# A recurrent-memory attention kernel with feed-forward: the memory rows turned by VectorE block transposes in place of TensorE matmuls

## The chip, the cores and the metric

The kernel runs on one core of one Trainium2 chip. A core has TensorE (PE in the profile; its weight loads are PEld), VectorE (DVE), ScalarE (ACT), GpSimd (POOL) and SyncE (SP), which issues most of the transfers. Each engine works through its own instructions in order, and semaphores make one wait for another. The metric is the device time of one execution in microseconds (us), the median of several runs.

## The reference, cut to what matters

Attention runs over 64 segments of 32 tokens. Ahead of each segment stand 8 memory rows, which are the first 8 output rows of the segment before: a recurrence. A feed-forward part follows.

```python
B, S, Dm = 1, 2048, 640; H, Dh = 32, 128; M, seg = 8, 32
mask = (idx[:, None] < M) | (idx[:, None] >= idx[None, :])
mem = mem0
for s in range(64):
    h = concat([mem, x[:, s*32:(s+1)*32]], axis=1)          # 40 rows
    q, k, v = h @ Wq, h @ Wk, h @ Wv                        # 32 heads of 128
    p = softmax(where(mask, q @ k.T * Dh**-0.5, -1e9))
    o = (p @ v) @ Wo
    mem = o[:, :M]                                          # 8 rows to the next segment
    outs.append(o[:, M:])
h  = x + A(layernorm(x))
h2 = h + (relu(layernorm(h) @ w1 + b1)**2 @ w2 + b2)
```

Only the 8 memory rows tie a segment to the next.

## The kernel before

One step of the main loop (`step(b, sp)`, four to a block `b` of 128 tokens) handles one segment. 24 of its 32 tokens ("main") share a stationary tile with the 8 memory rows: `hT4` holds, for each of the 5 chunks of 128 features and each of the 4 segments of a block, 32 columns, first 8 memory rows, then 24 main tokens. The other 8 tokens of a segment ("tail") are collected over 16 segments and projected in units (`tail_units`) that are put into gaps: the list `fill` holds such units (a unit is 4 matmuls), and `run(fill, n)` issues n of them. The lists `late`, `mid` and `win` hold other work for three places of a step. The order is written by hand; every engine follows it.

A step goes so:

- Projections of queries and keys for 16 heads at a time (`project`, `proj`, L204). ScalarE evacuates a product (`row`), VectorE turns it in 32x32 blocks (`flip`, L225, L396) into `qT` and `kT`. `qT` has 40 columns for each head: 8 memory queries, 24 main, 8 tail.
- `spread` (L362, L364) copies on POOL the memory queries out of `qT` into `qz`; the memory queries' scores (`scores`, L409) read `qz`. The token scores (`token_scores`, L485) read the columns `M:NK` of `qT`: main and tail queries.
- Projection of the values, the softmax of the memory scores (`soft1`, `soft2`, with the transpose `pTm`, L428), then the values of the tokens of the step before (`token_values`) and of this step's memory queries (`values`, L437 and L442), evacuated to `oT` by `values_out` (L211, L213).
- The place `win`: in the fourth step of a block (`sp == 3`) `ln_transpose` turns the 128 rows of the block after the next with five 128x128 matmuls (L179), and ScalarE copies them to a new `hT4` (L190). Then two `fill` units, the token softmax, and `wo_rounds` (L236), 64 matmuls with `oT` as stationary tile into `pw`.
- ScalarE copies half of `pw` (`otmp`, L243), VectorE adds both halves (`o`, L244): 8 memory rows and, below them, 24 main rows of the step before, for both halves of the output's columns (partitions 0 to 31 and 32 to 63). `wov2` picks the columns that go to each half: pieces of 64.
- Five more `fill` units, then `mem_to_hT` (L305): 20 small matmuls against the identity turn the memory rows into `pm` (L308), and VectorE copies `pm` to the first 8 columns of the next segment's tile (`hT`, L310). `tails_in` copies on POOL the next segment's tail queries into `qT` (L314) and its tail keys into `kT` (L315).
- `mid`, the rest of `fill`, and the transposes `pTt` (L555) and `pTk` (L561) of the token softmax for the next step. Then the next step's projections, whose stationary tile is `hT`.

`store_main` writes the main rows to DRAM (L330). The first step is different: its projections are streamed with the arriving weights (`start`), and its tail values `vt` are loaded by POOL's queue (L326). The feed-forward part follows the loop.

Of the kernel before, what the change touches and what calls it, by code (L numbers as in the profile page):

```python
# [16 lines left out]
def kernel(  # L17
# [16 lines left out]
    nc = tc.nc  # L34
# [49 lines left out]
    nc.gpsimd.affine_select(out=mask[0:32], in_=mask[0:32], compare_op=ALU.is_ge, fill=NEG, base=0,  # L84
# [13 lines left out]
    qT = const.tile([128, H, NK], BF16)  # L98
# [31 lines left out]
    for o in o_ring:  # L130
        nc.gpsimd.memset(o[64:128], 0.0)
# [3 lines left out]
    for ch in range(2):  # L135
        nc.sync.dma_start(out=o0[32 * ch:32 * ch + M, :].rearrange("m (c f) -> m c f", f=64),
                            in_=A_mem0[0].rearrange("m (c t f) -> t m c f", t=2, f=64)[ch])
# [22 lines left out]
    hT4s, hTts, tails = {}, {}, {}  # L160
# [13 lines left out]
    def ln_transpose(b):  # L174
# [6 lines left out]
        def out():  # L181
# [6 lines left out]
            hT4 = s2.tile([128, DC, 4, SEG], BF16, tag="hT4", name="hT4")  # L188
            ptv = pt[:, 0:640].rearrange("p (c s t) -> p c s t", c=DC, s=4)
            nc.scalar.copy(out=hT4[:, :, :, M:SEG], in_=ptv[:, :, :, 0:HD])  # L190
            hT4s[b] = hT4
# [35 lines left out]
    wov2 = wo[:].rearrange("p h (c t f) -> p h t c f", t=2, f=64)  # L227
# [76 lines left out]
    def mem_to_hT(o, hT4, sp):  # L304
        pm = chn.tile([128, 512], F32, tag="ch", name="pm")  # L305
        for c in range(DC):
            for q in range(4):
                nc.tensor.matmul(pm[32 * q:32 * q + 32, c * M:(c + 1) * M], lhsT=o[:, (2 * c + q % 2) * 32:(2 * c + q % 2 + 1) * 32],  # L308
                                 rhs=ident[:, q // 2 * 32:q // 2 * 32 + M], start=True, stop=True)
        nc.vector.tensor_copy(out=hT4[:, :, sp, 0:M], in_=pm[:, 0:DC * M].rearrange("p (c m) -> p c m", m=M))  # L310

    def tails_in(b, sp):
        q, k = [tails[b][w][:].rearrange("p h (k s) -> p h s k", s=4)[:, :, sp, :] for w in "qk"]
        nc.gpsimd.tensor_copy(out=qT[:, :, SEG:NK], in_=q)  # L314
        nc.gpsimd.tensor_copy(out=kT[:, :, SEG:2 * SEG].rearrange("p h (j k) -> p h j k", k=TL),  # L315
                              in_=k.unsqueeze(2).to_broadcast([128, H, 4, TL]))

# [10 lines left out]
    def store_main(o, s):  # L328
        for ch in range(2):
            nc.sync.dma_start(out=o_all[s * SEG:s * SEG + HD, ch * DH:(ch + 1) * DH],  # L330
                              in_=o[32 * ch + M:32 * ch + 32, :])
# [4 lines left out]
    def token_values(s, v, vt4, po):  # L336
# [8 lines left out]
        for u in range(2):  # L345
            for g in range(G):
                r = slice(32 * g, 32 * g + 32)
                nc.tensor.matmul(po[:, g, u * 128:(u + 1) * 128].rearrange("p (j q) -> p j q", q=32)[:, :, HD:32],
# [19 lines left out]
    def step(b, sp, v=None):  # L368
# [82 lines left out]
        if not last and not ready:  # L451
            spread(0)
# [419 lines left out]
```

## Time and profile before

| | |
|---|---|
| median of 3 runs | 1040.73 us (1040.03 to 1041.76) |
| span of the profiled execution | 1035.5 us |
| mean granted TensorE clock in it | 0.993 |
| first projection after the first step's end to that after the 63rd | 70.18 to 886.12 us |
| a plain step | 12.85 us |

The span runs from the first to the last instruction. A row of a timeline gives start, duration, engine, line and operation; x is the number of instructions merged into it, and brackets hold how long the engine was idle before and what released it. A row of a group gives line, engine, operation, out<-in, shapes and count, then busy time in us, the mean of one in ns, and the idle time before it. These groups belong to the parts that the diff touches:

```profile
L308 PE MATMUL pm<-ident,o 128*32 128x8 bf16 x1280 | 18.6, 169 | 13.1 <-DVE o L244 12.3
L310 DVE CAST hT<-pm 128x40 bf16<-128x40 f32 x64 | 12.7, 199 | 27.4 <-PE pm L308 27.4
L314 POOL COPY qT<-qTt 128x256 bf16<-128x256 bf16 x64 | 27.5, 430 | 0.8 <-DVE qTt L225 0.8
L362 POOL COPY qz<-qT 128x96 bf16<-128x96 bf16 x126 | 33.4, 265 | 125.0 <-DVE qT L225 121.5 <-DVE mx L415 3.6
L179 PE MATMUL pt<-ident,xn 128*128 128x128 bf16 x100 | 10.0, 234 | 10.9 <-DVE xn L170 8.6 <-ACT row L220 2.1
L190 ACT COPY hT<-pt 128x480 bf16<-128x480 bf16 x16 | 8.7, 543 | 5.3 <-PE pt L179 5.3
```

### The profile page before, as it was taken

The page shows a single profiled execution, that of the slowest core. Times are in us where ns is not written, and L with a number is a line of the kernel's source. Part 1 is how long each engine was busy: PE and PEld are TensorE (multiplying, and loading weights), DVE is VectorE, ACT ScalarE, POOL GpSimd, SP SyncE. Part 2 cuts the span into 40 slices and gives each one's busy share as a digit, 9 for nine tenths or more (in the row PEclk, how much of TensorE's full clock was granted, in tenths as well). Part 3 has the DMA queues.
Part 4 walks back from the last instruction along what each step waited for, and adds up shares of the span by engine and source line. Part 5 has one row for each costly group of instructions (what it writes and reads, how often), then busy time and mean ns, then how long its engine had stood idle before and what let it go on. Part 6 is the DMA issues. An engine that isn't in the chain of part 4 may idle for free.

```text
span 1035.5 us, 58905 instructions
## 1 busy us (share of the span) xinstructions
PE 980.1 (95%) x26960; PEld 563.9 (54%) x26960; DVE 621.6 (60%) x1740; ACT 536.0 (52%) x1225; POOL 312.3 (30%) x805
## 2 busy tenths in 40 slices
PE   5879899999999999999999999999999998999998
PEld 2335455555655555555555655555555555555565
DVE  2155666766566666666666666666666676565432
ACT  2435555555555555555555555555555555534431
POOL 1033333333333333332333233333333333343210
PEclk9889999999999999999999999999999999999999
DMA  8960101000100000000000000000000110612200
GB/s 319 405 205 26 22 7 31 7 24 6 32 10 22 15 24 24 16 20 14 26 15 22 15 27 15 22 15 27 15 21 8 47 33 7 194 54 72 77 26 26
DMA packets 39112, 51.58 MB, mean 50 GB/s; under 512 B 6160, under 2 KB 34960, under 8 KB 36944
## 3 DMA queue, kind: packets, MB, share of 16 engines
q1 hardware_dynamic: 38000, 47.30, 13.8%
q8 instruction: 210, 3.44, 1.4%
q14 instruction: 38, 0.31, 0.1%
q10 hardware_dynamic: 544, 0.26, 0.1%
q0 software_dynamic: 320, 0.26, 0.1%
HBM read 38.37 MB, written 9.44 MB: 46 GB/s over the span
## 4 chain that ended last, share of the span: by engine, by line
PE 83%; DMA 6%; DVE 5%; issue 3%; ACT 2%; POOL 0%; SPq 0%; DVEq 0%; ACTq 0%; POOLq 0%
PE ps L204 45%; PE pw L236 13%; PE y L823 6%; PE ps L791 5%; PE ps L236 3%; DMA xt<-in_A_x_dram 3%; PE po L437 2%; PE pm L308 2%; PE sm L409 2%; DMA wq<-in_B_w_dram 1%; PE po L343 1%; PE ps L485 1%; ACT em L418 1%; DMA vt_d<-row 1%; DVE o L244 1%
## 5 line engine op out<-in xcount | busy, mean ns | idle before, releaser
L204 PEld LDWEIGHTS <-hT 128*32 128x32 bf16 x7680 | 186.9, 96 | 180.8 <-DVE hT L310 19.6
L204 PE MATMUL ps<-wv,hT 128*32 128x512 bf16 x2520 | 169.9, 379 | 0.7 <-ACT v L492 0.7
L236 PE MATMUL pw<-wo,oT 128*32 128x320 bf16 x4224 | 159.6, 300 | 3.3 <-DVE pTt L555 1.2
L204 PE MATMUL ps<-wq,hT 128*32 128x512 bf16 x2520 | 158.1, 380 | 4.8 <-DVE hT L310 4.8
L204 PE MATMUL ps<-wk,hT 128*32 128x512 bf16 x2520 | 157.6, 379 | 0.0
L236 PEld LDWEIGHTS <-oT 128*32 128x32 bf16 x4224 | 109.3, 97 | 50.7 <-DVE oT L211 15.8
L535 POOL TENSOR_TENSOR pkt<-ek,rk 128x64 bf16<-128x64 bf16 x64 | 18.8, 294 | 377.6 <-DVE rk L533 377.6
L220 ACT ACTIVATE row<-ps 128x512 bf16<-128x512 f32 x156 | 91.9, 601 | 78.4 <-PE ps L204 74.6
L225 DVE STREAM_TRANSPOSE qT<-row 128x512 bf16<-128x512 bf16 x128 | 90.6, 709 | 51.9 <-ACT row L220 51.9
L222 ACT CAST row<-ps 128x512 bf16<-128x512 f32 x115 | 65.9, 596 | 34.3 <-PE ps L204 34.3
L315 POOL COPY kT<-kTt 128x1024 bf16<-128x1024 bf16 x64 | 70.9, 1108 | 13.7 <-DVE kTt L225 13.7
L362 POOL COPY qz<-qT 128x96 bf16<-128x96 bf16 x126 | 33.4, 265 | 125.0 <-DVE qT L225 121.5
L353 ACT CAST oT<-po 128x512 bf16<-128x512 f32 x128 | 68.7, 589 | 1.6
L244 DVE TENSOR_TENSOR o<-pw,otmp 64x320 bf16<-64x320 f32 x66 | 31.8, 482 | 61.9 <-ACT otmp L243 61.9
L204 PEld LDWEIGHTS <-hTt 128*32 128x32 bf16 x1920 | 48.8, 99 | 35.6 <-issue 9.9
L225 DVE STREAM_TRANSPOSE kT<-row 128x512 bf16<-128x512 bf16 x65 | 46.0, 708 | 31.1 <-ACT row L222 31.1
L243 ACT COPY otmp<-pw 64x320 f32<-64x320 f32 x66 | 27.9, 422 | 70.9 <-PE pw L236 70.9
L823 PE MATMUL y<-wq,wk 128*128 128x320 bf16 x416 | 60.9, 299 | 0.0
L393 ACT CAST row<-ps 128x256 bf16<-128x256 f32 x126 | 40.7, 375 | 29.1 <-PE ps L204 29.0
L531 DVE TENSOR_REDUCE zk<-ek 128x8 f32<-128x320 bf16 x64 | 31.1, 486 | 40.2 <-ACT ek L527 40.2
L527 ACT ACTIVATE ek<-tk 128x320 bf16<-128x320 f32 x64 | 30.1, 470 | 45.1 <-DVE tk L525 45.1
L418 ACT ACTIVATE em<-sm,mx 128x64 bf16<-128x64 f32 x126 | 40.4, 321 | 24.3 <-DVE mx L415 24.3
(114 smaller groups left out, 1657.5 us busy)
## 6 DMA issues: line engine op xcount, KB each, us to landing
wv<-in_A_Wv_dram SPq DMA_DIRECT2D x5, 1024.0 KB
wq<-in_A_Wq_dram SPq DMA_DIRECT2D x5, 1024.0 KB
wk<-in_A_Wk_dram SPq DMA_DIRECT2D x5, 1024.0 KB
wo<-in_A_Wo_dram SPq DMA_DIRECT2D x4, 1280.0 KB
vt<-vt_d SPq DMA_DIRECT2D x60, 64.0 KB
xt<-in_A_x_dram SPq DMA_DIRECT2D x20, 160.0 KB
vt_d<-row SPq DMA_DIRECT2D x22, 128.0 KB
wq<-in_B_w_dram SPq DMA_DIRECT2D x1, 2080.0 KB
```

The source lines that it names most:

```text
L204: nc.tensor.matmul(ps[32 * k:32 * k + 32, :], lhsT=lhs(c), rhs=wr[:, c, n, k], start=(c == 0), stop=(c == DC - 1))
L220: nc.scalar.mul(out=row, in_=ps, mul=scale)
L222: nc.scalar.copy(out=row, in_=ps)
L225: nc.vector.transpose(out=dst[:, n * 16:(n + 1) * 16, 0:32], in_=row.rearrange("p (h e) -> p h e", e=32))
L236: nc.tensor.matmul(pw[32 * j:32 * j + 32, 0:DH], lhsT=lhs(p), rhs=wov2[:, head(p), ch], start=(h == 0), stop=(h == 15))
L244: nc.vector.tensor_tensor(out=o[0:64], in0=pw[0:64, 0:DH], in1=tmp[0:64], op=ALU.add)
L315: nc.gpsimd.tensor_copy(out=kT[:, :, SEG:2 * SEG].rearrange("p h (j k) -> p h j k", k=TL), in_=k.unsqueeze(2).to_broadcast([128, H, 4, TL]))
L353: nc.scalar.copy(out=oTg[:, n, :, :, M:NK], in_=po[:, :, n * 128:(n + 1) * 128].rearrange("p g (j q) -> p g j q", q=32))
L393: nc.scalar.copy(out=row[:, u * 256:(u + 1) * 256], in_=ps[:, u * 256:(u + 1) * 256])
L418: nc.scalar.activation(out=em[:], in_=sms[n][:, 0:2 * SEG], func=ACT.Exp, bias=mx[:, 0:1], scale=1.0, accum_out=zm[:])
L791: nc.tensor.matmul(ps[:], lhsT=w1[:, c, fc * 128:(fc + 1) * 128], rhs=hnT[:, c, :], start=(c == 0), stop=(c == DC - 1))
L823: nc.tensor.matmul(y[:, hh, 0:DH], lhsT=f1T[:, fc, k * 128:(k + 1) * 128], rhs=w2[:, fc, cs], start=(fc == 0), stop=False, skip_group_chec ...
```

## The change

- The stationary tiles of all blocks become one tile `hTall`, with an offset of 24 columns: for each chunk of features two blocks of four segments of 32 columns (8 memory, 24 main). `mem_to_hT` now runs straight behind `o` and consists of two VectorE transposes of 64 partitions by 160 elements, one for each half of a chunk's 128 partitions. Each writes 32 columns in every chunk: the 8 memory columns of the next segment and the 24 columns ahead of them, which hold the main tokens of the segment that has just been worked through.
- For that the rows of `o` are in another order: 24 main rows, then 8 memory rows, and its columns are dealt to the two halves in pieces of 32. `wo_rounds` therefore reads the columns `M:NK` of `oT`, `oT` keeps the memory columns last, `wov2`, `prep_sum`, `store_main` and the load of `mem0` follow.
- Tail queries take the memory queries' place in `qT`, which shrinks to 32 columns: `tails_q_in` copies them on POOL for 16 heads at a time, behind `spread`. The mask and the positions in `pTt`, `po` and `oT` follow (tail queries first, then main).
- Since the transposes overwrite main columns, `ln_transpose` for the next block moves from the fourth step of a block to the first step of the one after, and that of the tail rows from a first step to a second.
- The five memsets of `o`'s lower half go, as nothing reads it any more.

```diff
     nc.vector.memset(mask[:], 0.0)
-    nc.gpsimd.affine_select(out=mask[0:32], in_=mask[0:32], compare_op=ALU.is_ge, fill=NEG, base=0,
+    nc.gpsimd.affine_select(out=mask[0:32], in_=mask[0:32], compare_op=ALU.is_ge, fill=NEG, base=-TL,
+                            pattern=[[0, HG], [-1, SEG]], channel_multiplier=1)
+    nc.gpsimd.memset(mask[0:TL], 0.0)
+    nc.gpsimd.affine_select(out=mask[0:TL], in_=mask[0:TL], compare_op=ALU.is_ge, fill=NEG, base=HD,
                             pattern=[[0, HG], [-1, SEG]], channel_multiplier=1)
...
     nc.vector.tensor_scalar(out=bmask[:], in0=same[:], scalar1=-1.0, scalar2=-NEG, op0=ALU.add, op1=ALU.mult)
-    qT = const.tile([128, H, NK], BF16)
+    qT = const.tile([128, H, SEG], BF16)
+    hTall = const.tile([128, HD + DC * 2 * 4 * SEG], BF16, name="hTall")
     kT = const.tile([128, H, 2 * SEG], BF16)
...
     o_ring = [const.tile([128, DH], BF16, name="o%d" % k) for k in range(5)]
-    for o in o_ring:
-        nc.gpsimd.memset(o[64:128], 0.0)
     o0 = o_ring[-1]
...
     for ch in range(2):
-        nc.sync.dma_start(out=o0[32 * ch:32 * ch + M, :].rearrange("m (c f) -> m c f", f=64),
-                            in_=A_mem0[0].rearrange("m (c t f) -> t m c f", t=2, f=64)[ch])
+        nc.sync.dma_start(out=o0[32 * ch + HD:32 * ch + 32, :].rearrange("m (a f) -> m a f", f=32),
+                            in_=A_mem0[0].rearrange("m (a t f) -> t m a f", t=2, f=32)[ch])
     load_tail_rows(0)
...
 
-    hT4s, hTts, tails = {}, {}, {}
+    hTts, tails = {}, {}
+    hTv = hTall[:, HD:].rearrange("p (c b s t) -> p c b s t", c=DC, b=2, s=4)
+
+    def rows_of(b, sp):
+        return lambda c: hTv[:, c, b % 2, sp, :]
     xns = {}
...
                 return
-            hT4 = s2.tile([128, DC, 4, SEG], BF16, tag="hT4", name="hT4")
             ptv = pt[:, 0:640].rearrange("p (c s t) -> p c s t", c=DC, s=4)
-            nc.scalar.copy(out=hT4[:, :, :, M:SEG], in_=ptv[:, :, :, 0:HD])
-            hT4s[b] = hT4
+            nc.scalar.copy(out=hTv[:, :, b % 2, :, M:SEG], in_=ptv[:, :, :, 0:HD])
         return out
...
 
-    wov2 = wo[:].rearrange("p h (c t f) -> p h t c f", t=2, f=64)
+    wov2 = wo[:].rearrange("p h (a t f) -> p h t a f", t=2, f=32)
 
...
 
-    def mem_to_hT(o, hT4, sp):
-        pm = chn.tile([128, 512], F32, tag="ch", name="pm")
-        for c in range(DC):
-            for q in range(4):
-                nc.tensor.matmul(pm[32 * q:32 * q + 32, c * M:(c + 1) * M], lhsT=o[:, (2 * c + q % 2) * 32:(2 * c + q % 2 + 1) * 32],
-                                 rhs=ident[:, q // 2 * 32:q // 2 * 32 + M], start=True, stop=True)
-        nc.vector.tensor_copy(out=hT4[:, :, sp, 0:M], in_=pm[:, 0:DC * M].rearrange("p (c m) -> p c m", m=M))
+    def mem_to_hT(o, b, sp):
+
+        at = (b % 2 * 4 + sp) * SEG
+        hc = hTall[:, 0:DC * 8 * SEG].rearrange("p (c r) -> p c r", c=DC)
+        for u in range(2):
+            ov = o[0:64].rearrange("p (c u f) -> p u c f", u=2, f=32)[:, u]
+            nc.vector.transpose(out=hc[64 * u:64 * u + 64, :, at:at + SEG], in_=ov)
 
     def tails_in(b, sp):
-        q, k = [tails[b][w][:].rearrange("p h (k s) -> p h s k", s=4)[:, :, sp, :] for w in "qk"]
-        nc.gpsimd.tensor_copy(out=qT[:, :, SEG:NK], in_=q)
+        k = tails[b]["k"][:].rearrange("p h (k s) -> p h s k", s=4)[:, :, sp, :]
         nc.gpsimd.tensor_copy(out=kT[:, :, SEG:2 * SEG].rearrange("p h (j k) -> p h j k", k=TL),
...
 
+    def tails_q_in(b, sp, n):
+        q = tails[b]["q"][:].rearrange("p h (k s) -> p h s k", s=4)[:, n * 16:(n + 1) * 16, sp, :]
+        nc.gpsimd.tensor_copy(out=qT[:, n * 16:(n + 1) * 16, 0:TL], in_=q)
+
     vt4s = {}
...
             nc.sync.dma_start(out=o_all[s * SEG:s * SEG + HD, ch * DH:(ch + 1) * DH],
-                              in_=o[32 * ch + M:32 * ch + 32, :])
+                              in_=o[32 * ch:32 * ch + HD, :])
 
...
                 r = slice(32 * g, 32 * g + 32)
-                nc.tensor.matmul(po[:, g, u * 128:(u + 1) * 128].rearrange("p (j q) -> p j q", q=32)[:, :, HD:32],
+                nc.tensor.matmul(po[:, g, u * 128:(u + 1) * 128].rearrange("p (j q) -> p j q", q=32)[:, :, 0:TL],
                                  lhsT=vt4[r, sp, u, :], rhs=pTx[r, u], start=False, stop=True, skip_group_check=True)
...
         for n in range(2):
-            nc.scalar.copy(out=oTg[:, n, :, :, M:NK],
+            nc.scalar.copy(out=oTg[:, n, :, :, 0:SEG],
                            in_=po[:, :, n * 128:(n + 1) * 128].rearrange("p g (j q) -> p g j q", q=32))
-        nc.gpsimd.tensor_copy(out=oTts[s // 4 % 2][:, :, s % 4 * TL:(s % 4 + 1) * TL], in_=oT[:, :, 32:NK])
+        nc.gpsimd.tensor_copy(out=oTts[s // 4 % 2][:, :, s % 4 * TL:(s % 4 + 1) * TL], in_=oT[:, :, 0:TL])
 
...
         last = s == NS - 1
-        hT4 = hT4s[b]
-        lhs = lambda c: hT4[:, c, sp, :]
+        lhs = rows_of(b, sp)
         ready = v is not None
...
                 c0 = 256 + n * 4 * M
-                evac(n == 0, oTg[:, n, :, :, 0:M], po[:, :, c0:c0 + 4 * M].rearrange("p g (j m) -> p g j m", m=M))
+                evac(n == 0, oTg[:, n, :, :, SEG:NK], po[:, :, c0:c0 + 4 * M].rearrange("p g (j m) -> p g j m", m=M))
 
...
             spread(0)
+        tails_q_in(b, sp, 0)
         if not last:
...
             spread(1)
+        tails_q_in(b, sp, 1)
 
...
                 for g in range(G):
-                    nc.tensor.matmul(skv[32 * g:32 * g + 32, n * 4 + j, :], lhsT=qT[:, n * 16 + g * 4 + j, M:NK],
+                    nc.tensor.matmul(skv[32 * g:32 * g + 32, n * 4 + j, :], lhsT=qT[:, n * 16 + g * 4 + j, :],
                                      rhs=kT[:, n * 16 + g * 4 + j, 0:NK], start=False, stop=(n == 1 and j == 3),
...
         pw = chn.tile([128, 512], F32, tag="ch", name="pw")
-        wo_rounds(lambda p: oT[:, p, 0:32], pw, 0, 16)
+        wo_rounds(lambda p: oT[:, p, M:NK], pw, 0, 16)
         o = wo_out(pw)
+        if not last:
+            mem_to_hT(o, (s + 1) // 4, (s + 1) % 4)
         if s:
...
             run(fill, 5)
-            mem_to_hT(o, hT4s[(s + 1) // 4], (s + 1) % 4)
             tails_in((s + 1) // 4, (s + 1) % 4)
...
         for u in range(2):
-            nc.gpsimd.tensor_tensor(out=pTx[:, u], in0=pTt[:, u, HD:32].unsqueeze(1).to_broadcast([128, 4, TL]),
+            nc.gpsimd.tensor_tensor(out=pTx[:, u], in0=pTt[:, u, 0:TL].unsqueeze(1).to_broadcast([128, 4, TL]),
                                     in1=same[:], op=ALU.mult)
...
         ot, fx = got
-        fv = fx.rearrange("p (c t f) -> p t c f", t=2, f=64)
-        nc.vector.tensor_tensor(out=fv, in0=ot.rearrange("p (t c f) -> p t c f", t=2, f=64), in1=fv, op=ALU.add)
+        fv = fx.rearrange("p (a t f) -> p t a f", t=2, f=32)
+        nc.vector.tensor_tensor(out=fv, in0=ot.rearrange("p (t a f) -> p t a f", t=2, f=32), in1=fv, op=ALU.add)
         return fx
...
         v = s2.tile([128, EG], BF16, tag="v", name="v")
-        main = lambda c: hT4s[0][:, c, 0, :]
+        main = rows_of(0, 0)
         units = []
...
     ln_transpose(0)()
-    mem_to_hT(o0, hT4s[0], 0)
+    mem_to_hT(o0, 0, 0)
     ln_norm(("t", 0))
...
                 mid.append(lambda b=b: ln_norm(b + 2))
-            if b + 2 < NB and sp == 3:
-                win.append(lambda b=b: ln_transpose(b + 2))
+            if 0 < b < NB - 1 and sp == 0:
+                win.append(lambda b=b: ln_transpose(b + 1))
             if b in (2, 6) and sp == 1:
...
                 tg = ("t", b // 4 + 2)
-            if b in (2, 6) and sp == 3:
+            if b in (3, 7) and sp == 0:
                 late.append(lambda tg=tg: ln_stats(tg))
                 mid.append(lambda tg=tg: ln_norm(tg))
-            if b in (3, 7) and sp == 0:
+            if b in (3, 7) and sp == 1:
                 win.append(lambda tg=tg: ln_transpose(tg))
...
         pw = chn.tile([128, 512], F32, tag="ch", name="pw")
-        wo_rounds(lambda p: oT[:, p, 0:32], pw, 0, 16)
+        wo_rounds(lambda p: oT[:, p, M:NK], pw, 0, 16)
         store_main(wo_out(pw), s)
```

## The prediction

> **What bounds the kernel now.** I read the page's shares and its chain of waits first, then the timeline around the end of one step, then the groups by form, then the same place in other steps.
>
> ```profile
> PE 980.1 (95%) x26960; PEld 563.9 (54%) x26960; DVE 621.6 (60%) x1740; ACT 536.0 (52%) x1225; POOL 312.3 (30%) x805
> ...
> PE 83%; DMA 6%; DVE 5%; issue 3%; ACT 2%; POOL 0%; SPq 0%; DVEq 0%; ACTq 0%; POOLq 0%
> ```
>
> TensorE looks like the bound almost everywhere. But a matmul record includes the time until its result is out, so short waits hide inside "busy". The end of a step shows them (start, duration, engine, line; this is the end of the 34th step).
>
> ```profile
> 503.53 0.48 DVE L244 TENSOR_TENSOR o<-pw,otmp 64x320 bf16<-64x320 f32 x1 [0.73 <-ACT otmp L243]
> ...
> 504.07 0.29 PE L308 MATMUL pm<-ident,o 128*32 128x8 bf16 x20
> ...
> 504.21 0.60 PE L204 MATMUL ps<-wq,hTt 128*32 128x512 bf16 x8
> 504.45 0.20 DVE L310 CAST hT<-pm 128x40 bf16<-128x40 f32 x1 [0.43 <-PE pm L308]
> ...
> 504.70 0.62 PE L204 MATMUL ps<-wq,hT 128*32 128x512 bf16 x8
> 504.92 0.24 DVE L555 STREAM_TRANSPOSE pTt<-pkt 128x64 bf16<-128x64 bf16 x1
> 505.08 0.40 DVE L561 STREAM_TRANSPOSE pTk<-pk 128x256 bf16<-128x256 bf16 x1
> ```
>
> The 20 filling matmuls ahead of `pm` start at 502.80 and need 54 ns each (in the timeline the 20 of `wq` start at 504.70 and the next 20 at 505.79), so they are issued by 503.89; `pm` starts at 504.07, when `o` is ready. The 8 fillers behind it are issued by 504.65; the projection starts at 504.70, 0.05 behind `hT`. So the chain `pw`, `otmp`, `o`, `pm`, `hT`, projection sets the step here, and TensorE waits in it. From the end of `o` to the first projection I get 0.690 us on average in 49 of the 63 step ends: 0.06 to `pm`, 0.12 to its last issue, 0.45 to the end of `hT`, 0.055 to TensorE. In the other 14 (the fourth step of a block, with 16 fillers behind `pm`) it is 0.735.
>
> **The change, part by part.**
>
> *The memory rows.* Removed: 64 x 20 matmuls and 64 casts. Added: two transposes of 64 partitions x 160 elements, straight behind `o`. No row has that size; the neighbours are
>
> ```profile
> L428 DVE STREAM_TRANSPOSE pTm<-pmem 128x64 bf16<-128x64 bf16 x126 | 30.9, 245 | 4.3
> ...
> L561 DVE STREAM_TRANSPOSE pTk<-pk 128x256 bf16<-128x256 bf16 x64 | 25.7, 402 | 0.0
> ```
>
> Half way between 64 and 256 elements lies 160: (245 + 402) / 2 = 324 ns. Bounds: from 512 elements at 669 ns (the undisturbed `qTt` flips) to 256 at 402 the slope is 1.04 ns an element; down from 402 that gives 302 ns, up from 245 it gives 345. I take 324, as both neighbours count equally. The second starts before the first is over: `pTk` starts at 505.08 and the next flip at 505.40, 0.08 before its end. A dependent VectorE instruction starts 0.034 behind its source (`tk` behind `mxk`, all 64 steps). New gap: 0.034 + (2 x 0.324 - 0.076) + 0.055 = 0.661 us; 0.617 at the low bound, 0.703 at the high one.
>
> Gain: 49 x (0.690 - 0.661) + 14 x (0.735 - 0.661) = 1.4 + 1.0 = 2.4 us; 5.2 at the low bound, a loss of 0.2 at the high one. The 0.14 us of issue that `pm` held on TensorE (504.07 to 504.21) is not a gain of its own: the fillers end that much earlier and TensorE waits longer for the transposes. VectorE is free again 0.606 behind `o` instead of 0.635, so `xn`, `pTt` and `pTk` are not later.
>
> The overlap matters. [...]
>
> *Tail queries.* The POOL copy of 256 elements (430 ns) leaves the end of the step; two of 128 come behind `qz`. Rows of 96 and 256 elements (265 and 430 ns) give some 0.30 each. The second has its data at 510.07 (end of `qz`) and is over by 510.45; its reader, the second half of the token scores, is issued at 511.03. Cover 0.6 us, and the first half has over a microsecond: nothing. Behind the copies POOL has only `pkt`, which waited 5.8 us for VectorE. `kT` and `pTx` come 0.43 earlier, for nobody who waits. In the first step the copies stand ahead of the four POOL loads of `vt`:
>
> ```profile
> 55.03 1.08 POOL L315 COPY kT<-kTt 128x1024 bf16<-128x1024 bf16 x1 [13.69 <-DVE kTt L225]
> 56.06 0.83 POOL L326 DMA_DIRECT2D vt<-vt_d  x1
> ```
>
> There the chain runs through that load, so two copies cost 0.5 us once (0 if the DMA engines, 90% and more busy until 63, swallow it; 0.6 at most).
>
> *The turn of the next 128 rows* (five 128x128 matmuls, one ScalarE copy) moves from the fourth step of a block to the first of the next. Before, with it and without it:
>
> ```profile
> 473.73 0.18 PE L437 MATMUL po<-pTm,v 32*128 32x8 bf16 x3 [0.45 <-issue]
> 473.74 0.21 PE L442 MATMUL po<-pTm,vt 32*128 32x32 bf16 x4
> 473.88 0.45 PE L179 MATMUL pt<-ident,xn 128*128 128x128 bf16 x5
> 474.26 0.59 PE L236 MATMUL ps<-wo,oTt 128*32 128x320 bf16 x12
> 474.68 0.31 PE L236 MATMUL pw<-wo,oT 128*32 128x320 bf16 x4
> ```
>
> ```profile
> 840.84 0.20 PE L442 MATMUL po<-pTm,vt 32*128 32x32 bf16 x4
> 840.96 0.59 PE L236 MATMUL ps<-wo,oTt 128*32 128x320 bf16 x12
> 841.45 2.36 PE L236 MATMUL pw<-wo,oT 128*32 128x320 bf16 x64
> ```
>
> With it `pw` starts 0.37 behind the evacuated `oT`, without it 0.05: 13 fourth steps give back 0.32 each, 4.2 us. The first steps of blocks 4 to 14 have 8 fillers in that place; with a turn among them (the tail rows of block 7) `pw` starts 0.40 behind, so 11 steps pay 0.35, 3.9 us; blocks 1 to 3 have no fillers and pay nothing. Net -0.3 (bounds: -4.2 if the first steps hide it, +3.9 if the fourth steps don't give it back; the two readings of the same place exclude both). The two turns of tail rows move into steps of the same kind, with the same 1.6 us ScalarE copy: nothing.
>
> *Fetching.* The first line above shows a hole of 0.45 us with no visible cause. 20-odd such holes lie at matmul numbers with the same remainder by 128, and the page's instruction queue has 210 packets for 26,960 matmuls, 128 each. Over a plain step of 12.85 us the steps hold 19.2 us; 4.7 (13 x 0.36) and 1.3 are the turns, 13 the holes. The changed program has 2,560 of 53,922 TensorE instructions less: -0.6 us, give or take 1.5 for where the holes fall.
>
> *Without a price:* `wo` read in pieces of 32 elements (`wq`, read so, runs 380 ns a matmul, `wv` in pieces of 128 runs 379); the memory load in twice the pieces (its issue took 0.69 to 0.85 us, the bias load of 1,664 two-byte pieces 0.43, so pieces don't set it); the mask and five memsets, while POOL waited 0.9 us for VectorE.
>
> Sum: -2.4 - 0.3 - 0.6 + 0.5 = -2.8 us. The profiled span of 1035.53 becomes 1032.7; the median of the runs lies 5.2 us above that span, so 1040.73 becomes 1037.9. A difference under 0.2% (2.1 us) is what a measurement here can't tell from none.
>
> **Rivals.**
> 1. *A draw:* the transposes cost the high bound (345 ns) or the holes fall badly. 0.2 - 0.3 - 0.6 + 0.5 = -0.2, time 1040.5, with 1.5 for the holes 1039 to 1042. For it: the gain per step is 0.03 us. Against: it needs the worst of both rows.
> 2. *Slower, VectorE does not overlap the pair:* 0.034 + 0.648 + 0.055 = 0.737 per step end, 49 x 0.047 = 2.3 lost, nothing in the other 14; with the rest 1040.73 + 2.3 - 0.4 = 1042.6. It decides from 300 ns a transpose without overlap, or 338 with it. For it: two operations pay their fixed part twice, and half of the `kT` flips of 256 took 447 ns, not 402; against: every pair of flips in the timeline overlaps, and POOL, which was busy beside the slow ones, stands still from 503.81 to 504.66.
> 3. *TensorE's own time counts:* 63 x 0.14 = 8.8 us less, with 0.5 for the start 1032.4. Against: the projection waits for `hT` in every step end.
> 4. *The tail queries are late:* from 0.6 us more than priced, per step. A copy would have to take 0.9 us. At 1.0 us, 63 x 0.1 = 6.3 less the 2.8 above: 1044.
>
> That the change does not do what it says is excluded: its TensorE program is shorter by exactly these 2,560 instructions.
>
> **How the numbers follow.** Forecast 0.48, rival 1 0.25, rival 2 0.18, rival 3 0.06, rival 4 0.03. Faster: 0.48 + 0.06 = 0.54; same 0.25; slower 0.18 + 0.03 = 0.21. The forecast's own range is 1035.5 (302 ns) to 1038.6. The range that should hold the time reaches half way into rival 3 and past the price of rival 2: 1034.0 to 1043.0.
>
> **What would show it.** Each step: the transposes at 0.30 to 0.345 us, the second starting 0.24 behind the first; `o` to projection 0.66 in all 63 step ends, with no second value for fourth steps. The turn: `pw` 0.05 behind `oT` in fourth steps and 0.40 in first ones from block 4. Fetching: fewer holes. Tail queries: no TensorE wait on POOL. I am wrong if a transpose takes over 340 ns, if the pair doesn't overlap, or if TensorE waits at the token scores.

## The result, and the profile after

The changed kernel takes 1050.52 us (median of 4 runs, 1050.20 to 1052.44), the kernel before on the same chip 1040.38 (4 runs, 1039.10 to 1041.76). The ratio is 1.0095, 95% interval 1.0079 to 1.0112: slower by 10 us, where 1037.9 was forecast.

The page of the changed kernel, TensorE's and VectorE's shares and the engines on the chain that ended last:

```profile
PE 964.3 (92%) x25671; PEld 562.9 (54%) x25680; DVE 656.6 (62%) x1804; ACT 536.5 (51%) x1225; POOL 326.0 (31%) x866
...
PE 75%; DVE 10%; DMA 5%; issue 4%; ACT 4%; POOL 0%; SPq 0%; ACTq 0%; DVEq 0%; POOLq 0%
```

TensorE has 16 us less work, as the removed matmuls say, and its share of the chain has gone from 83% to 75%; VectorE's has doubled. TensorE waits for VectorE: for `hTall` 34.9 us in all, where the kernel before waited 12.3 for `o` and 4.8 for `hT`. The end of a step in the timeline (start, duration, engine, line; idle time before in brackets):

```profile
511.64 1.68 PE L208 MATMUL ps<-wq,hTt 128*32 128x512 bf16 x28
...
511.92 0.42 ACT L247 COPY otmp<-pw 64x320 f32<-64x320 f32 x1 [1.03 <-PE pw L240]
...
512.38 0.48 DVE L248 TENSOR_TENSOR o<-pw,otmp 64x320 bf16<-64x320 f32 x1 [0.73 <-ACT otmp L247]
...
512.89 0.69 DVE L314 STREAM_TRANSPOSE hTall<-o 64x160 bf16<-64x160 bf16 x2
...
513.61 0.47 DVE L176 TENSOR_SCALAR xn<-xt,lnmv,lnrs 128x640 bf16<-128x640 bf16 x1
513.63 1.05 PE L208 MATMUL ps<-wq,hTall 128*32 128x512 bf16 x16 [0.31 <-DVE hTall L314]
```

The two transposes take 0.69 us from 512.89: in single records 0.336 and 0.339 us, the second starting 0.014 behind the end of the first. They don't overlap, and `xn` behind them does not either: it starts 0.03 behind their end. The projection starts 0.05 behind the second, 0.78 behind the end of `o`. So it is in the 63 step ends (0.777 to 0.781, and 0.836 in one). Summed over the 62 steps from the first projection of the second step to that of the last, this distance is 48.3 us, against 43.4 before: **4.9 us of the loss**.

The rest is elsewhere. The waits of TensorE, one line of the changed kernel's list, and the same of the kernel before (total, times, longest):

```profile
PE po L443 <- issue: 7.3, 23, 0.6
```

```profile
PE po L437 <- issue: 1.8, 6, 0.5
```

The matmuls of the memory queries' values stand still 23 times where nothing that they need is late. One of them in the timeline of the changed kernel, between the 16 matmuls of line 443 and the 4 of line 448:

```profile
346.83 0.37 PE L350 MATMUL po<-pTk,v 32*128 32x32 bf16 x32
347.05 0.24 PE L355 MATMUL po<-pTx,vt 32*128 32x32 bf16 x8
347.12 0.29 PE L443 MATMUL po<-pTm,v 32*128 32x8 bf16 x16
347.25 0.20 PE L448 MATMUL po<-pTm,vt 32*128 32x32 bf16 x4
347.45 0.26 PE L443 MATMUL po<-pTm,v 32*128 32x8 bf16 x16
348.28 0.20 PE L448 MATMUL po<-pTm,vt 32*128 32x32 bf16 x4 [0.56 <-issue]
```

Short matmuls are issued here, mostly under 10 ns apart, and then comes a hole of more than half a microsecond. Call a hole the excess over the median distance of the same two lines, where the trace shows nothing that was waited for. If all recorded matmuls of the program are numbered in order of time, from 0, all 37 holes of over 0.25 us of the changed kernel between 75 and 900 us lie ahead of a number with remainder 94 by 128; so do 25 of the 26 of the kernel before. The page's instruction queue has a packet for each 128 matmuls:

```profile
q8 instruction: 200, 3.28, 1.3%
```

200 packets for 25,671 matmuls and 25,680 weight loads, 16.4 KB each: one for a block of 128 matmuls with their weight loads. The holes are at the boundaries between these blocks.

The times of these packets in the trace show the same. In the kernel before and in the changed one there are 380 boundaries between 75 and 900 us, and at all but three of them exactly as many packets had landed as boundaries had been passed before: one packet for each block. The changed kernel has an excess of over 0.25 us at 41 of its boundaries; in 39 of them the latest packet had landed 1.24 to 1.56 us before the block's first matmul (median of the 41: 1.39). Where the excess was under 0.1 us, it had landed 3.5 us before (median). The next packet starts 1.13 us behind the hole (median), and a packet takes 1.07. So, as an estimate, a block that is wanted less than 1.13 + 1.07 + 1.39 = 3.6 us after the one before it comes late.

What a boundary costs goes in these runs with how fast the block before it was issued. The mean excess at a boundary, by the time in which the 128 matmuls ahead of it were issued (number of boundaries in brackets):

| time of 128 matmuls | before | changed | `after_wo4`, below |
|---|---|---|---|
| under 2.0 us | 0.49 (2) | 0.54 (3) | 1.11 (9) |
| 2.0 to 2.5 us | 0.46 (7) | 0.47 (17) | 1.09 (53) |
| 2.5 to 3.0 us | 0.21 (34) | 0.29 (40) | 0.54 (43) |
| 3.0 to 3.5 us | 0.06 (40) | 0.28 (3) | 0.17 (30) |
| 3.5 to 4.0 us | 0.00 (15) | 0.08 (14) | 0.11 (14) |
| 4.0 to 5.0 us | 0.03 (37) | 0.09 (28) | 0.06 (18) |
| over 5 us | 0.03 (61) | 0.01 (79) | 0.03 (43) |

128 matmuls in less than 3 us occur in one stretch of a step only: token scores, values, and the output product. Such a block ends 220 to 340 matmuls behind the step's first projection, mostly 240 to 300. A plain step before has 400 matmuls, 16 more than 3 x 128, so the boundary wanders through the step and is in that stretch in some steps only. A plain step of the changed kernel has 380, and four steps in a row hold 1529 (380 + 380 + 404 + 365) or 1549, where 12 x 128 is 1536: the boundary stays. In the 54th to the 61st step it stood 247, 251, 255, 235, 254, 258, 262 and 242 matmuls behind the first projection, with holes of 0.2 to 0.8 us in seven of the eight. All holes of over 0.1 us at the boundaries together: 16.1 us before, 24.6 changed, **8.5 us of the loss**.

4.9 and 8.5 are 13.4; the loop of 62 steps is 12.4 us longer (828.4 against 815.9), as other parts of it give back 1.0. The start is 2.6 us later, behind the loop both take 149.4. That makes the difference of the two profiled spans, 1050.6 and 1035.5. The medians are 10.1 apart: the profiled execution of the changed kernel was its slowest (1052.44, 1.8 over its span), while that of the kernel before was a fast one: other executions of it took 2.1 to 2.2 more than their spans, which puts it at some 1037.7, 2.7 below its median.

### The profile page after: what moved, and what is told of

The parts are those of the page before. It is cut to its first block, busy times and chain, and to the rows that moved or that the text cites. A ratio compares the mean times of both kernels' runs of the same rounds, so it can differ in the third digit from the quotient of the medians.

```text
span 1050.6 us, 56335 instructions
## 1 busy us (share of the span) xinstructions
PE 964.3 (92%) x25671; PEld 562.9 (54%) x25680; DVE 656.6 (62%) x1804; ACT 536.5 (51%) x1225; POOL 326.0 (31%) x866
## 4 chain that ended last, share of the span: by engine, by line
PE 75%; DVE 10%; DMA 5%; issue 4%; ACT 4%; POOL 0%; SPq 0%; ACTq 0%; DVEq 0%; POOLq 0%
PE ps L208 41%; PE pw L240 14%; PE y L832 5%; PE ps L800 5%; DVE hTall L314 3%; DVE o L248 3%; DMA xt<-in_A_x_dram 3%; ACT otmp L247 3%; PE po L443 2%; PE sm L415 2%; PE po L350 1%; PE ps L240 1%; PE ps L493 1%; DMA wq<-in_B_w_dram 1%; DMA vt<-vt_d 1%
## 5 line engine op out<-in xcount | busy, mean ns | idle before, releaser
L208 PEld LDWEIGHTS <-hTall 128*32 128x32 bf16 x7680 | 188.6, 96 | 221.1 <-DVE hTall L314 62.4
L208 PE MATMUL ps<-wq,hTall 128*32 128x512 bf16 x2520 | 158.5, 380 | 35.4 <-DVE hTall L314 34.9
L208 PE MATMUL ps<-wv,hTall 128*32 128x512 bf16 x2520 | 170.0, 379 | 0.7 <-ACT v L500 0.7
L240 PE MATMUL pw<-wo,oT 128*32 128x320 bf16 x4224 | 157.4, 300 | 1.9 <-DVE pTt L564 1.2
L208 PE MATMUL ps<-wk,hTall 128*32 128x512 bf16 x2520 | 157.9, 379 | 0.0
L318 POOL COPY kT<-kTt 128x1024 bf16<-128x1024 bf16 x64 | 74.6, 1165 | 13.7 <-DVE kTt L229 13.7
L208 PEld LDWEIGHTS <-hTt 128*32 128x32 bf16 x1920 | 51.0, 99 | 42.7 <-issue 7.5
```

Of the source, the lines that this page charges most:

```text
L208: nc.tensor.matmul(ps[32 * k:32 * k + 32, :], lhsT=lhs(c), rhs=wr[:, c, n, k], start=(c == 0), stop=(c == DC - 1))
L240: nc.tensor.matmul(pw[32 * j:32 * j + 32, 0:DH], lhsT=lhs(p), rhs=wov2[:, head(p), ch], start=(h == 0), stop=(h == 15))
```

## The experiments

Two theories stood at the start: the place of the fetch boundary and the transposes (theory A), or the transposes and nothing else (theory B).

**Moving the boundary, nothing else.** Some small matmuls on TensorE ahead of everything shift every later matmul against the blocks. They cost under 0.01 us each, once (96 of them are issued in 0.7 us).

```diff
+    pad = chn.tile([128, 512], F32, tag="ch", name="pad")
+    for i in range(48):
+        nc.tensor.matmul(pad[32 * (i % 4):32 * (i % 4) + 32, 0:8], lhsT=ident[:, 0:32],
+                         rhs=ident[:, 0:8], start=True, stop=True)
     ln_stats(0)
```

Four kernels: the changed one with 48, 96 and 128 of them, where 128 is the control (a whole block, so the boundaries stand where they stood), and the kernel before with 48.

> 48 small matmuls into an unused accumulator stand ahead of everything else on TensorE, which is idle there until 5.8 us; nothing else is changed. Theory A (fetching): holes come every 128 matmuls; a step of the changed kernel has 380 matmuls, nearly 3 x 128, so the hole returns to the same place of each step, the values between token_values and oT (about 45 of 63 steps, 0.2 to 0.8 us each). 48 matmuls more move the boundary from position 239 to 289 in a step to 191 to 241, where the kernel before shows no holes: 12 to 17 us less, 1034 to 1039. Theory B (the two transposes that do not overlap, 0.78 us instead of 0.69 from o to the projection, are the loss, and holes only move about): 1049 to 1052.

> The same with 96 matmuls. Theory A: the middle boundary of a step falls at 143 to 193 (no holes in the kernel before), but the third at 271 to 321, where that kernel shows holes of 0 to 0.5 us: between the other two, 1040 to 1048. Theory B: 1049 to 1052.

> Control: 128 matmuls, a whole period, so the boundary falls where it did. Theory A: as the changed kernel, 1049 to 1052, although most matmuls are added here. Theory B: 1049 to 1052 too. A time far from this would mean that the added matmuls act in another way (the clock, the start).

> The kernel before with 48 matmuls ahead. Its steps have 400 matmuls, so the boundary moves 16 places a step and passes every position. Theory A: the holes land in other steps, but about as many: 1037 to 1044. Theory B: 1039 to 1042.

Measured, with the kernel before at 1039.72 on that chip (holes of over 0.1 us at the boundaries from 75 to 900 us, loop as above, both of the profiled execution):

| kernel | median us | ratio to before, 95% | holes us | loop us |
|---|---|---|---|---|
| changed, 48 | 1044.14 | 1.0046 (1.0031 to 1.0062) | 13.8 | 821.3 |
| changed, 96 | 1058.92 | 1.0189 (1.0162 to 1.0215) | 31.6 | 837.5 |
| changed, 128 | 1052.91 | 1.0124 (1.0094 to 1.0154) | 25.6 | 830.1 |
| before, 48 | 1049.15 | 1.0087 (1.0061 to 1.0114) | 20.5 | 823.3 |

The control is where the changed kernel is, and has its holes at the same line. 48 matmuls make the changed kernel 9 us faster than 128, 96 make it 6 us slower, and the kernel before loses 9 us by 48. Theory B falls: it has the same time for the first three, and no change for the fourth. Theory A keeps its mechanism, as the place of the boundary does change the time, but none of its four ranges held: 48 was expected at 1034 to 1039, 128 at 1049 to 1052. For 96 (1040 to 1048) it had the direction wrong too, and for the kernel before (1037 to 1044, about as many holes) it saw no change where there was one. For 48 I had forgotten that the 4.9 us of the transposes stay. For 96 the boundary comes into the output product, with 13.3 us of holes there. The kernel before, unpadded, turns out to stand at a good place: with 48 its holes are 4.4 us more. The other 5 us of that run are not the holes: its start came 1.8 us later, the part behind the loop took 2.2 more, and one early step lost 3.2 us, of which 1.7 in a wait for `qz` (2.2 us, 0.5 without the 48), as POOL stood 4.2 us ahead of it for the load of the biases. Whether the 48 matmuls bring these about was not followed.

**The transposes undone, and the best place.** In `after_pm` the memory rows are turned by 20 matmuls and a cast again, in the interleaved tile; the tail queries and the turn of the next rows stay as changed. The cut leaves out that the call moves back behind the five `fill` units and that the five memsets of `o` return.

```diff
+        pm = chn.tile([128, 512], F32, tag="ch", name="pm")
+        for c in range(DC):
+            for q in range(4):
+                nc.tensor.matmul(pm[32 * q:32 * q + 32, c * M:(c + 1) * M],
+                                 lhsT=o[:, (2 * c + q // 2) * 32:(2 * c + q // 2 + 1) * 32],
+                                 rhs=ident[:, q % 2 * 32 + HD:q % 2 * 32 + 32], start=True, stop=True)
+        nc.vector.tensor_copy(out=hTv[:, :, b % 2, sp, 0:M], in_=pm[:, 0:DC * M].rearrange("p (c m) -> p c m", m=M))
-        for u in range(2):
-            ov = o[0:64].rearrange("p (c u f) -> p u c f", u=2, f=32)[:, u]
-            nc.vector.transpose(out=hc[64 * u:64 * u + 64, :, at:at + SEG], in_=ov)
```

> The transposes alone undone: the memory rows turned by 20 TensorE matmuls and a cast again, behind five fillers as before, everything else of the change kept (interleaved stationary tile, tail queries ahead, turn of the next rows moved). Steps have 400 matmuls again. Theory A (fetching plus the transposes make the loss): o-end to projection 0.69 us again in most step ends (43 to 45 us over 62, against 48.3), holes at the fetch boundary 13 to 18 us, time 1039 to 1043. Theory B (another part of the change makes the loss): 1047 or more.

It took 1040.29 us (10 runs; before 1040.24 in 18; ratio 1.0006, 0.9990 to 1.0022). From `o` to the projection 43.2 us in the loop, holes 18.2, loop 815.0. So the loss comes with the transposes: with their wait, and with the 20 matmuls that they took out of each step. The tail queries, the tile and the moved turn together cost nothing that can be measured. The place of the turn shows what was forecast for it: from the half of `oT` that VectorE evacuates to the output product the fourth steps of a block went from 0.378 to 0.097 us on average, the first ones from 0.095 to 0.342.

`after_k36` is the changed kernel with 36 small matmuls ahead, the edit as above.

> The changed kernel with 36 small matmuls on TensorE ahead of everything: the fetch boundary moves by 36 matmuls in every step. Replaying the recorded starts of the changed kernel with the boundary moved gives holes of some 6 us for 36, 7 for 48, 18 for 0. Theory A (fetching): 1 to 2 us below the run with 48 (1044.1), 1041 to 1044, and the distance o-end to projection stays at 0.78. Theory B (only the transposes): 1050 to 1052 with the control of 128.

1042.66 us (10 runs; ratio 1.0017, 1.0001 to 1.0033), as expected of theory A. Holes 13.1, loop 817.3, and the distance from `o` to the projection still 48.4. The place of the boundary alone is thus worth some 10 us (1052.91 with 128, 1042.66 with 36); of the loop's 12.8 us between these two, the holes are 12.5. What is left of the loss is 2.4: 4.9 for the transposes, less 3.0 for holes that are now fewer than in the kernel before, would be 1.9.

**Why the pair does not overlap.** Kernels with VectorE's transposes alone, in chains of four between memsets. Three of the seven, cut to what matters (`k` counts the instructions; each writes columns of its own):

```python
        elif n == "te":
            nc.vector.transpose(out=ds[0:64], in_=ss[0:64])
        elif n == "tf":
            nc.vector.transpose(out=ds[64:128], in_=ss[0:64])
        else:                                                # tg: in turn, as the changed kernel does
            u = k % 2
            nc.vector.transpose(out=d[:].rearrange("p (c r) -> p c r", c=5)[64 * u:64 * u + 64, :, k // 2 * 32:k // 2 * 32 + 32],
                                in_=(ss, ss1)[u][0:64])
```

> VectorE block transposes alone, 160 elements a partition, in chains of four between memsets: ta 128 partitions, contiguous; tb 64 partitions, contiguous; tc 128 partitions, source in pieces of 32; td 128 partitions, destination in pieces of 32 that lie 256 apart; te 64 partitions, both in pieces; tf the same with the destination on partitions 64 to 127; tg alternating as the kernel does. Everything that the reference computes is left out. Theory A (the pair does not overlap because a transpose of 160 elements on VectorE has a fixed part that the next cannot enter, whatever its shape): 330 to 345 ns for each in all seven chains, starts 0.345 to 0.355 apart. Theory B (the pieces of 32 or the 64 partitions cost the overlap): ta, or ta and tb, have their starts 0.05 to 0.09 closer than te, tf and tg.

The timeline of that kernel, three of the seven chains (a chain's four instructions are one line: start of the first, time to the end of the last):

```profile
5.13 0.97 DVE L67 STREAM_TRANSPOSE te<-src 64x160 bf16<-64x160 bf16 x4
6.06 0.09 DVE L77 MEMSET fin<- 128x32 uint32 x1
6.18 1.02 DVE L69 STREAM_TRANSPOSE tf<-src 64x160 bf16<-64x160 bf16 x4
7.27 0.09 DVE L77 MEMSET fin<- 128x32 uint32 x1
7.27 1.35 DVE L72 STREAM_TRANSPOSE tg<-src 64x160 bf16<-64x160 bf16 x4
```

`te` takes 0.97: each starts 0.226 to 0.232 behind the one before, 0.064 ahead of its end. (Each chain runs twice in the one execution; the distances from start to start agree to 0.002 us, the overlap of `te` is 0.074 the second time.) `ta` to `td` are the same to 0.02. `tf` overlaps in itself too. Only the alternating `tg` takes 1.35: 0.35 from start to start, 0.014 behind the end, the numbers of the changed kernel. Both theories fall. Neither the pieces of 32, nor the 64 partitions, nor the length cost the overlap in these chains; going from one half of the partitions to the other does. What exactly must differ, the next kernel asked.

> VectorE alone again, 160 elements a partition, contiguous, in chains of four. Transposes: ua source and destination both on partitions 0 to 63, then both on 64 to 127, in turn; ub source 0 to 63 and 64 to 127 in turn, destination 0 to 63; uc across, 0 to 63 into 64 to 127 and back; ud all 128 and 0 to 63 in turn. Copies: ue 0 to 63 into itself; uf 0 to 63 into 0 to 63 and 64 to 127 in turn; ug 0 to 63 into 64 to 127. Everything that the reference computes is left out. Theory 1 (the overlap is lost where an instruction shifts its rows to other partitions by another distance than the one before): ua, ud, ue and ug start 0.226 apart and before the end of the one before (copies at their own distance), ub, uc and uf 0.35 apart and behind its end. Theory 2 (it is lost wherever the destination goes to another half): ua is lost too, ub is not. Theory 3 (it concerns transposes alone): uf overlaps like ue.

```profile
1.32 1.36 DVE L60 STREAM_TRANSPOSE ua<-src 64x160 bf16<-64x160 bf16 x4
...
2.87 1.40 DVE L62 STREAM_TRANSPOSE ub<-src 64x160 bf16<-64x160 bf16 x4
...
5.67 0.98 DVE L67 STREAM_TRANSPOSE ud<-src 128x160 bf16<-128x160 bf16 x4
...
6.62 0.49 DVE L69 COPY ue<-src 64x160 bf16<-64x160 bf16 x4
...
7.07 0.78 DVE L71 COPY uf<-src 64x160 bf16<-64x160 bf16 x4
```

`ua` loses the overlap though it shifts nothing (against theory 1), `ub` loses it though its destination stays (against theory 2), and the copies `uf` lose it like transposes (against theory 3): 0.207 from start to start, where `ue` has 0.110. `ud`, 128 and 64 partitions in turn, both from partition 0, keeps it. What all fourteen chains have in common: an instruction starts ahead of the end of the one before, by 0.06 to 0.08 us, when its source and its destination each start at the same partition as that one's; if either starts elsewhere, it starts 0.014 us behind the end, and a transpose's record is some 0.04 longer (0.336 us in the changed kernel, 0.296 in `te`). The chains start at partitions 0 and 64 only; no run shows other places.

**Fewer instructions behind `o`.** Two versions need one transpose of 128 partitions. In `after_wo4` the output product goes in 128 matmuls of 160 columns into four groups of 32 partitions, so that nothing has to be added.

```diff
-                    nc.tensor.matmul(pw[32 * j:32 * j + 32, 0:DH], lhsT=lhs(p), rhs=wov2[:, head(p), ch],
+                    nc.tensor.matmul(pw[32 * q:32 * q + 32, 0:DQ], lhsT=lhs(p), rhs=wov2[:, head(p), q],
...
-        nc.scalar.copy(out=tmp[0:64], in_=pw[64:128, 0:DH])
-        nc.vector.tensor_tensor(out=o[0:64], in0=pw[0:64, 0:DH], in1=tmp[0:64], op=ALU.add)
+        nc.vector.tensor_copy(out=o[:], in_=pw[:, 0:DQ])
...
+        nc.vector.transpose(out=hc[:, :, at:at + SEG], in_=o[:].rearrange("p (c f) -> p c f", f=32))
```

> The output product of the step in 128 matmuls of 160 columns (was 64 of 320), all of K into each of the four quadrants, so that no halves are added: one VectorE cast from PSUM and one transpose of 128 partitions take the place of a ScalarE copy, an add and two transposes. If two transposes that follow each other cost twice the whole and partitions cost nothing: transpose 0.34 us once, o-end to projection 0.43 where TensorE waits, the chain from pw to the projection 1.0 to 1.1 us less. The 28 fillers there need 1.5 us, so TensorE sets the step end: 0.2 to 0.4 us less per step, 12 to 25 us, against holes of up to 0.45 per step where the 128 matmuls of the product are issued in 2.4 us: 1025 to 1048 us. If a transpose of 128 partitions costs more than one of 64 (0.45 us or more): 1045 or more.

1108.35 us (4 runs; ratio 1.0646, 1.0609 to 1.0684), far outside. The chain did get shorter: the time from the start of the last matmul of `pw` to the end of `o` fell from 83.3 us in the loop to 37.2. But the output product itself, from the start of its first matmul to that of its last, grew from 128.5 to 194.9. The group of its matmuls, with the idle time before them:

```profile
L240 PE MATMUL pw<-wo,oT 128*32 128x160 bf16 x8448 | 173.8, 234 | 54.1 <-issue 52.9 <-DVE oT L216 0.4 <-DVE o L246 0.4
```

52.9 us of `issue`, against 0.2 in the changed kernel. A step, in the timeline:

```profile
531.16 1.77 PE L240 MATMUL pw<-wo,oT 128*32 128x160 bf16 x92
533.85 0.81 PE L240 MATMUL pw<-wo,oT 128*32 128x160 bf16 x36 [0.92 <-issue]
```

92 matmuls in 1.8 us, a boundary, and nothing for 0.92 us. The holes at the boundaries sum to 97.5 us. That fits the fetching theory with a larger dose: the same columns in twice the instructions. At all 102 boundaries with an excess of over 0.25 us the block's packet had landed 1.21 to 1.56 us before its first matmul.

In `after_one` the product keeps its 64 matmuls. Those of the second half of K read their two groups of columns in reverse order, so that partitions 0 to 63 and 64 to 127 of `pw` hold what one add of 128 partitions needs; the crossed halves are copied first.

```diff
+                    rhs=wov2[:, head(p), ch, ::(-1 if kh else 1)],          # columns as (u, c, f)
...
-        nc.scalar.copy(out=tmp[0:64], in_=pw[64:128, 0:DH])
-        nc.vector.tensor_tensor(out=o[0:64], in0=pw[0:64, 0:DH], in1=tmp[0:64], op=ALU.add)
+        nc.vector.tensor_copy(out=tmp[64:128], in_=pw[0:64, DQ:DH])
+        nc.scalar.copy(out=tmp[0:64], in_=pw[64:128, DQ:DH])
+        nc.vector.tensor_tensor(out=o[:], in0=pw[:, 0:DQ], in1=tmp[:], op=ALU.add)
```

> One transpose of 128 partitions in place of the pair. The output product keeps its 64 matmuls; those of the second half of K read the two groups of columns in the other order (a negative stride), so that the halves are crossed: VectorE and ScalarE each copy 64 rows x 160 side by side, one add of 128 x 160, one transpose. Theory (the pair cost its second transpose and its lost overlap): o-end to projection 0.43 us where TensorE waits, instead of 0.78. From the end of pw to the projection 1.2 to 1.3 us instead of 1.83, under which 28 fillers need 1.5, so TensorE's fillers set the step end and each of 62 steps gains about 0.3: 19 us less than the changed kernel at the same place of the fetch boundary, 1032, give or take 10 for where the holes fall. If reading backwards costs TensorE time: the output product above 2.4 us, 1050 or more.

> The same with 36 small matmuls on TensorE ahead, the best place of the fetch boundary for the changed kernel by the replay: 1042.7 less 19 = 1024, 1020 to 1034. If the chain behind pw sets nothing any more because the fillers do, and the holes move: up to 1040. If only the place of the boundary mattered and the pair of transposes did not: 1042.

`after_one` took 1046.43 (4 runs; before 1041.39 in 7; ratio 1.0054, 1.0033 to 1.0075), `after_one_k36` 1032.45 (4 runs; ratio 0.9919, 0.9895 to 0.9943): faster than both kernels. The end of a step of the latter:

```profile
511.59 1.70 PE L209 MATMUL ps<-wk,hTt 128*32 128x512 bf16 x28
...
511.82 0.32 DVE L248 COPY otmp<-pw 64x160 f32<-64x160 f32 x1 [0.35 <-PE pw L241]
...
512.23 0.29 ACT L249 COPY otmp<-pw 64x160 f32<-64x160 f32 x1 [1.52 <-DVE otmp L248]
...
512.55 0.33 DVE L250 TENSOR_TENSOR o<-pw,otmp 128x160 bf16<-128x160 f32 x1 [0.41 <-ACT otmp L249]
...
512.91 0.34 DVE L314 STREAM_TRANSPOSE hTall<-o 128x160 bf16<-128x160 bf16 x1
513.18 0.20 DVE L564 STREAM_TRANSPOSE pTt<-pkt 128x64 bf16<-128x64 bf16 x1
...
513.31 0.40 DVE L570 STREAM_TRANSPOSE pTk<-pk 128x256 bf16<-128x256 bf16 x1
```

One transpose of 128 partitions costs here what one of 64 did (0.34 us), and `pTt` behind it starts 0.07 ahead of its end, where `xn` behind the pair started 0.03 after theirs. The time lies in the range that was expected, 8 us above the 1024 that it was worked out to be. From `o` to the projection 0.434 us, as expected, 27.7 in the loop where `after_k36` has 48.4. The two copies were meant to go side by side; they stand one behind the other, so it takes 87.1 us in the loop from `pw` to `o` (counted as above), not 83.6. Net 17.2, and the loop is 15.9 shorter than that of `after_k36` (801.4 against 817.3). The profiled span gains 9.2 (the medians differ by 10.2), because the start came 2.7 us later in that execution and the part behind the loop takes 3.9 more (154.2 against 150.3; four stores of `o` a step in place of two put SyncE's queue on the chain with 1%; that was not followed further). `after_one` missed its 1032: its loop is only 12.2 shorter than the changed kernel's, as its holes grew from 24.6 to 29.0 us, and the part behind the loop takes 6.5 more (155.9 against 149.4), 5.3 of it in one wait of TensorE that the changed kernel does not have. That a shorter wait ahead of the fast stretch makes the holes longer at a bad place of the boundary would fit, but no run separates it.

## Why the prediction was wrong, point by point

- **"The second starts before the first is over"** is the step that failed for the transposes. The price of one was near: 324 ns forecast, 337 measured. The overlap of 0.076 was read off `pTk` and the flip behind it, which start at partition 0 both; the pair goes to partitions 0 and 64. The gap became 0.034 + 0.336 + 0.014 + 0.339 + 0.055 = 0.778 us where 0.661 stood: 4.9 us lost, not 2.4 gained. Had both started at the same partition, chain `tf`, whose first record is as long as the pair's (0.339), gives 0.034 + 0.268 + 0.296 + 0.055 = 0.653, an estimate: a gain of some 3 us over the 43.4.
- **Rival 2**, that VectorE does not overlap the pair, was right about the pair with 0.18. It was too small in price (0.737, with 324 ns and no gap between the two, where the pair took 0.336 + 0.014 + 0.339), and its "nothing in the other 14" was wrong: they went from 0.735 to 0.782 on average. The runs show both cases: `te` and `ud` start 0.063 to 0.076 us before the end of the one before, the pair, whose destination goes from partition 0 to 64, 0.014 behind it.
- **"Fetching: -0.6 us, give or take 1.5 for where the holes fall"** is the step that failed most: the holes grew by 8.5. The prediction had found the holes and their remainder by 128, and then counted them in proportion to the instructions. What counts is where in a step the boundary stands, and taking 20 matmuls out of 400 parks it in the fast stretch. The bound of 1.5 had no row behind it; with 48 matmuls ahead and nothing else the holes of the kernel before grew by 4.4, those of the changed kernel fell by 10.8.
- *The turn of the next 128 rows* (-0.3): right, place by place (`after_pm`: fourth steps -0.28, first steps +0.25).
- *Tail queries* (nothing in the loop): right. The copies take 0.30 us, as taken, and no matmul of the token scores waits for them. Rival 4 is out.
- *The start* (+0.5): can't be told. It was 2.6 us later in the profiled execution. But the first projection of the second step stands between 70.2 and 74.0 us in the eleven profiled executions, in no order of the edits, and the profiled one of the kernel before is the earliest.
- *Without a price* (tile, masks, load): nothing, by `after_pm`.
- Rival 3, TensorE's own time: out. Its work fell by 16 us, and its waits for the memory rows grew from 17.1 us (for `o` and `hT`) to 34.9 (for `hTall`).
- A slip of no weight: with 302 ns a transpose the sum gives 1040.73 - 5.2 - 0.4 = 1035.1 as the low end of the forecast's own range, not 1035.5.

## What to carry to other kernels

Before two VectorE instructions are put behind each other on the critical chain, look at which partition each starts: from the same one they overlapped here by 0.07 us, from another one the second started 0.014 us behind the end of the first, and the pair of transposes cost 0.69 us in place of some 0.56 (0.268 + 0.296, estimated from `tf`). One transpose of 128 partitions cost the same 0.34 as one of 64.

Where TensorE issues many short matmuls, as in this kernel, with one instruction packet for each 128 (200 for 25,671), count them in blocks of 128: an edit that changes the number of matmuls in the loop's body moved the block boundary, and its place alone was worth up to 16 us (1058.92 with 96 matmuls ahead, 1042.66 with 36). So compare two versions each with several counts of idle matmuls ahead before the edit itself is judged.

Splitting matmuls finer at the same number of columns was not free: 64 more of them in a step brought 73 us more of holes (97.5 in `after_wo4`, 24.6 in the changed kernel).

## What the runs showed of the hardware

- One instruction packet of 16.4 KB landed for each 128 matmuls with their weight loads: 200 for 25,671 in the changed kernel, 210 for 26,960 in the kernel before. When a block was issued in 2.0 to 2.5 us, the next was late by 0.46 us on average, by 1.09 in `after_wo4`, where fast blocks often follow each other; from 3.5 us on, by 0.11 us or less on average. A block's first matmul never came less than 1.1 us behind the landing of its packet, in all eleven executions; where it was late, 1.4 (median).
- In the fourteen chains of `micro_t` and `micro_t2` VectorE started an instruction 0.06 to 0.08 us ahead of the end of the one before when source and destination each started at the same partition as that one's, and otherwise 0.014 us behind it. They start at partitions 0 and 64 only.
- TensorE read the output weights with a negative stride at no visible cost: from the first to the last of its 64 matmuls, 130.9 us in the loop of `after_one_k36` against 131.1 in that of `after_k36`.
